# One load and two sets of mask transfers moved between queues in an attention and PReLU kernel

## The chip, the cores and the metric

The kernel runs on one core of a Trainium2 chip. The metric is the device time of one execution in microseconds (us). A core has five engines that matter here: TensorE (PE, with its weight loads shown as PEld), VectorE (DVE), ScalarE (ACT), GpSimd (POOL) and SyncE (SP), which issues transfers. Each engine works through its own instructions in order; an instruction that waits holds up everything behind it on that engine. Transfers (DMA) are issued by SP, ACT or POOL and run on 16 DMA engines that all of them share.

## The reference

Two stages follow each other. The first is linear attention with decay in blocks of 64 positions, for 4 batches, 8 heads, 768 positions and 64 elements a head; the second is a two-layer feed-forward network on the 3072 resulting rows of 512 elements, with 2048 hidden elements and a PReLU between the layers.

```python
for b in range(nb):
    qb, kb, vb = q[:, :, sl], k[:, :, sl], v[:, :, sl]
    intra = einsum('bhic,bhjc->bhij', qb, kb) * Dmask[None]      # lam ** (i - j), 0 above the diagonal
    intra = einsum('bhij,bhjd->bhid', intra, vb)
    inter = einsum('bhid,bhde->bhie', qb * lam_pow[None], kv_state)
    out[:, :, sl] = intra + inter
    kb_dec = kb * rev_pow[None]
    kv_state = lam_block * kv_state + einsum('bhsd,bhse->bhde', kb_dec, vb)
...
h = x @ w_in
g = maximum(h, 0) + alpha * minimum(h, 0)
return g @ w_out
```

## The kernel before

**Tiling.** The kernel works with blocks of L = 128 positions, two to a window of W = 256. There are NC = 6 chunks: chunk c covers window c // 2 of the batches 2 * (c % 2) and 2 * (c % 2) + 1. A chunk has four attention units, numbered n = 4 * c + 2 * bi + hh, one for each of its two batches (bi) and each half of the heads (hh). So units 16 to 19 are chunk 4, the last but one, and units 18 and 19 its second batch. Chunks 4 and 5 (c >= HC) lay their keys out by halves of a block rather than by even and odd positions, and need their own arrangement of the decay masks.

**One unit.** load brings q and k of a batch in as 32-bit floats (L82; for k of the last chunks in four transfers, L94), load_vh brings v, cast to 16 bits on the way, in two transfers for each half (L335). cast makes 16-bit q and k (L298 on ACT, L300 on VectorE, L302 on POOL), key_decayed multiplies k by its decay (L358), transposes(n, "D") turns q and k with one transposing transfer on SP's queue (L378, tile qkT), decayed multiplies the turned q by its decay on POOL (L422, tile qdT). A cluster(old, new) then runs on PE inter(old) (L442, needs qdT of the old unit), score_products(new) (L460 in the last chunks, L472 before; needs qkT of the new unit), intra(old) (L506) and state_products(new) (L526); masked(new) multiplies the scores by the decay mask on VectorE (L485 in the last chunks, L487 before), attended copies the result on ACT (L298) and states updates the running states (L555).

**The masks of the last chunks.** half_mask(hh) builds the mask for half hh of the heads out of the general one by four transfers from SBUF to SBUF (L257), 64 KB each: 32 rows by 4 by 128 floats, written to every second row. half_mask(0) writes into a fresh tile (hmask). half_mask(1) reads the general mask of the second half and writes over that of the first (dmask), so it must come after masked(14), the last user of that one. later_half(hh) finishes each with a copy on POOL (L264). masked(16) is the first to need the mask of half 0, masked(17) that of half 1.

**Feed-forward.** up(c, f) makes one of 16 groups of 128 hidden elements for the 512 rows of chunk c (four matmuls at L635, a Relu of the negative on ACT at L643, the PReLU on VectorE at L650); down(c, t, part, 4) adds a quarter of the second product for 128 rows (four matmuls at L663), and the last quarter ends with a copy on ACT (L676) and a store on SP's queue (L679). PE alternates between these and the clusters.

**What sets the order.** The order is written out by hand, one call after another (L827 to L1135), then by a table (plan) for chunks 3 to 5. Each call appends its instructions to the engines' queues at that place. The change lies at L1081 to L1121, where the attention of units 11 to 16 is interleaved with down of chunk 1 and up of chunk 2. On SP's queue stand there in turn: the transposes of unit 14, a store, half of q for units 16 and 17, four mask transfers, a store, the transposes of unit 15, q for units 18 and 19, four transfers of k for the same, the transposes of unit 16, a store, four mask transfers, the transposes of unit 17. The tiles of qkT rotate over three buffers, the 32-bit q and k over five.

Of the kernel before, what the change touches and what calls it, by code (L numbers as in the profile page):

```python
# [11 lines left out]
def kernel(  # L12
# [16 lines left out]
    nc = tc.nc  # L29
# [52 lines left out]
    def load(c, bi, x, half=None, queue="S"):  # L82

        pb, b = c // 2, 2 * (c % 2) + bi
        if (c, bi) not in raws:
            raws[c, bi] = {}
        if x not in raws[c, bi]:
            raws[c, bi][x] = raw_pool.tile([128, H, 2 * D], fp32, tag=f"{x}raw", name=f"{x}raw")
        heads = ds(0, H) if half is None else ds(4 * half, 4)
        i = "kqv".index(x)  # L90
        if x == "k" and c >= HC:
            for a in range(2):
                for f in range(2):
                    nc.sync.dma_start(  # L94
                        out=raws[c, bi][x][ds(64 * a, 64), heads, ds(D * f, D)],
                        in_=k[b, heads, ds(pb * W + L * a + 64 * f, 64), :].rearrange("h p d -> p h d"),
                    )
            return
        (nc.gpsimd if queue == "G" else nc.sync).dma_start(  # L99
            out=raws[c, bi][x][:, heads, :],  # L100
            in_=(k, q, v)[i][b, heads, ds(pb * W, W), :].rearrange("h (p e) d -> p h (e d)", e=2),
        )
# [39 lines left out]
    def bank_of(bank, name, dtype=fp32):  # L142
        pool = h_ps_pool if bank == "h" else ps
        return pool.tile([128, CH], dtype, tag=bank, name=name)
# [102 lines left out]
    def half_mask(hh):  # L247

        m = [dmask[:, x].rearrange("p l h a j -> p (l h) (a j)") for x in range(2)]
        if hh == 0:  # L250
            t = raw_pool.tile([128, H, 2 * D], fp32, tag="vraw", name="hmask")
            HM[0] = t.rearrange("p h d -> p (h d)")[:, 0:768].rearrange("p (x j) -> p x j", j=192)
        else:
            HM[1] = m[0]
        for a in range(2):
            for e in range(2):
                nc.sync.dma_start(  # L257
                    out=HM[hh][64 * a + e : 64 * a + 64 : 2, :, 0:L],
                    in_=m[hh][ds(64 * a, 32), :, ds(64 * (1 - e), L)],
                )  # L260

    def later_half(hh):

        nc.gpsimd.tensor_copy(  # L264
            out=HM[hh][:, :, L:192].rearrange("p x (e j) -> p x e j", e=2),
            in_=HM[hh][:, :, 0:L].rearrange("p x (e j) -> p x e j", e=2)[:, :, :, 0:32],
        )
# [28 lines left out]
    def copy_on(eng, out, in_):  # L296
        if eng == "A":
            nc.scalar.activation(out, in_, AF.Copy)  # L298
        elif eng == "V":
            nc.vector.tensor_copy(out=out, in_=in_)  # L300
        else:
            nc.gpsimd.tensor_copy(out=out, in_=in_)  # L302

    def raw_of(n):
        c, bi, hh = units[n]
        return {
            x + "16": t[:, ds(4 * hh, 4), :].rearrange("p h (e d) -> p e h d", e=2)
            for x, t in raws[c, bi].items()
        }

    def cast(n, name, eng):
        t = T.setdefault(n, {})
        if name == "v16":
            t[name] = v_of(n)
            c, bi, hh = units[n]
            copy_on(eng, t[name].rearrange("p h e d -> p h (e d)"), raws[c, bi]["v"][:, ds(4 * hh, 4), :])
            return
        if "qk16" not in t:
            t["qk16"] = half_pool.tile([128, 2, 2, 4, D], fp16, tag="qk16", name="qk16")
        copy_on(eng, t["qk16"][:, int(name == "k16")], raw_of(n)[name])  # L320
# [3 lines left out]
    def v_of(n):  # L324
        c, bi, hh = units[n]
        if (c, bi) not in V:
            V[c, bi] = v_pool.tile([128, H, 2, D], fp16, tag="v16", name="v16")
        return V[c, bi][:, ds(4 * hh, 4)]

    def load_vh(c, bi, a):  # L330

        for n in (4 * c + 2 * bi, 4 * c + 2 * bi + 1):
            T.setdefault(n, {})["v16"] = v_of(n)
        for f in range(2):
            nc.gpsimd.dma_start(  # L335
                out=V[c, bi][ds(64 * a, 64), :, f],
                in_=v[2 * (c % 2) + bi, :, ds((c // 2) * W + L * a + 64 * f, 64), :].rearrange("h p d -> p h d"),
            )
# [11 lines left out]
    def engine(x):  # L350
        return nc.gpsimd if x == "G" else nc.vector

    def key_decayed(n, eng="G"):
        hh = units[n][2]
        kr = raw_of(n)["k16"]
        decay = hdecay if units[n][0] >= HC else kdecay
        kdec = kv_pool.tile([128, 2, 4, D], fp16, tag="kdec", name="kdec")
        engine(eng).tensor_tensor(  # L358
            out=kdec,
            in0=kr,  # L360
            in1=decay[:, ds(4 * hh, 4), :].rearrange("p h e -> p e h").unsqueeze(3).to_broadcast([128, 2, 4, D]),
            op=ALU.mult,
        )
        T.setdefault(n, {})["kdec"] = kdec
# [8 lines left out]
    def transposes(n, eng, decay=True):  # L373

        t = T[n]
        qkT = qkt_pool.tile([128, 2, 2, 2, L], fp16, tag="qkT", name="qkT")
        if eng == "D":
            nc.sync.dma_start(  # L378
                out=qkT.rearrange("p x e h j -> p (x e h) j"),
                in_=t["qk16"].rearrange("p x e h d -> p (x e h d)"),  # L380
                transpose=True,
            )
        else:
            tp = ps.tile([128, 2, 2, 2, L], fp16, tag="tk", name="tp")
            for x in (1, 0):
                for e in range(2):
                    for hp in range(2):
                        nc.tensor.transpose(
                            tp[:, x, e, hp, :],
                            t["qk16"][:, x, e, ds(2 * hp, 2)].rearrange("p l d -> p (l d)"),  # L390
                            ident,
                        )
            copy_on(eng, qkT, tp)
            t["qps"] = tp[:, 0]
        t["qkT"] = qkT
        if decay:
            decayed(n)
# [19 lines left out]
    def decayed(n, eng="G"):  # L417
        c, bi, hh = units[n]
        t = T[n]
        qdT = qkt_pool.tile([128, 2, 2, L], fp16, tag="qdT", name="qdT")  # L420
        p = ds(64, 64) if c < 2 else ds(0, L)
        engine(eng).tensor_tensor(  # L422
            out=qdT[:, :, :, p],
            in0=(t["qps"] if eng == "P" else t["qkT"][:, 0])[:, :, :, p],
            in1=qdecay[:, hh, :, :, p],
            op=ALU.mult,
        )
        t["qdT"] = qdT
# [139 lines left out]
    def cluster(old, new, eng="A"):  # L568

        if old is not None:  # L570
            inter(old)
        if new is not None:
            score_products(new)
        if old is not None:
            intra(old)
        if new is not None:
            state_products(new, kv_acc, old is None)
            masked(new)
        if old is not None:
            attended(old, eng)  # L580
        if new is not None:
            states(new, kv_acc)
# [35 lines left out]
    G = {}  # L618
# [35 lines left out]
    def lhs(c, f, t):  # L654
        return g_of(c, f)[:, t // 2, t % 2, :]

    def down(c, t, part, nparts, bank="op"):
        if part == 0:
            O[c, t] = bank_of(bank, "o_ps")
        o_ps = O[c, t]  # L660
        n = NF // nparts
        for f in range(part * n, part * n + n):
            nc.tensor.matmul(  # L663
                o_ps,
                lhsT=lhs(c, f, t),
                rhs=w_out_sb[:, f, :],
                start=(f == 0),
                stop=(f == NF - 1),
            )
        if part == nparts - 1:  # L670
            store(c, t, o_ps, 0, DM)
            del O[c, t]
# [408 lines left out]
    transposes(14, "D", False)  # L1081
    down(1, 2, 3, 4, "h")
    load(4, 0, "q", 1)
    half_mask(0)
    cast(15, "k16", "G")
    cast(17, "q16", "G")
    load_vh(4, 0, 0)
    cluster(11, 12, "A")
# [7 lines left out]
    key_decayed(17, "G")  # L1096
    up(2, 2, None, "h")
    up(2, 0, None, "tk")
    load(4, 1, "q", None)
    cast(17, "k16", "G")  # L1100
    decayed(14, "G")
    cast(16, "k16", "G")
    load_vh(4, 1, 0)
    cluster(12, 13, "A")
    load(4, 1, "k", None)
    transposes(16, "D", False)
    down(1, 3, 2, 4, "op")
    up(2, 1, None, "h")
    load_vh(4, 1, 1)
    up(2, 15, None, "h")  # L1110
    up(2, 8, None, "tk")
    later_half(0)
    decayed(15, "G")
    key_decayed(16, "G")
    key_decayed(18, "G")
    cluster(13, 14, "A")
    down(1, 3, 3, 4, "op")
    half_mask(1)
    up(2, 10, None, "h")
    up(2, 13, None, "h")  # L1120
    up(2, 11, None, "op")  # L1121
# [116 lines left out]
```

## Time and profile before

| | |
|---|---|
| runs of before, median (lowest to highest) | 207.32 us (206.71 to 207.41), 3 runs |
| profiled execution | 206.72 us |
| its span, first to last instruction | 204.9 us |
| PE busy | 198.6 us, 97% of the span |
| VectorE, POOL, ACT busy | 154.9, 116.1, 113.8 us |
| granted TensorE clock | 1.00 |
| the chain that ended last | PE 86%, DMA 4%, VectorE 3%, SP's issues 3% |

Times in the views are counted from the first instruction. A row of a timeline has the start, the length, the engine, the line of the kernel, the operation, what is written and read, and the count; in brackets stands the engine's idle time just before and what ended it. "SPq" is SP's queue: its rows are the issuing of a transfer, not the transfer. The time "to landing" of a transfer runs from the start of its issue until all of its data is reported written; for some transfers the trace has none.

### The profile page before, as it was taken

Reading aid. Unit: us, or ns where it says so; the run is one execution under the profiler, and the core shown is the slowest. Engines: PE = TensorE matmul, PEld = TensorE weight load, DVE = VectorE, ACT = ScalarE, POOL = GpSimd, SP = SyncE. Lnnn points to the kernel's source line nnn. Section 1 sums busy time; section 2 is a strip of 40 time slices with the busy share of each in tenths; the row PEclk is TensorE's granted clock in tenths of the full one; section 3 lists DMA queues with packets and bytes.
Section 4 is the critical chain, followed back from the end, with each engine's and each line's share of the span. In section 5 each row is a group of like instructions: output and inputs, shape, how many; then the busy total and the mean of one; then the engine's idle time right before and its main releaser. Section 6 shows DMA issues by size and latency. Waiting matters only on the chain.

```text
span 204.9 us, 5641 instructions
## 1 busy us (share of the span) xinstructions
PE 198.6 (97%) x2271; PEld 121.2 (59%) x2271; DVE 154.9 (76%) x289; ACT 113.8 (56%) x212; POOL 116.1 (57%) x145
## 2 busy tenths in 40 slices
PE   7999999999999999999799999999999999999993
PEld 6776445556445465555454554467666666666883
DVE  6988889578789647899977679958888467675831
ACT  7986778144777118656486466654453544534320
POOL 8999893054478991299286957982085040553000
PEclk9999999999999999999999999999999999999999
DMA  5999999997999996899999995381001111011123
GB/s 165 278 196 234 248 264 207 234 293 230 230 261 282 201 231 156 226 154 218 180 242 140 263 151 79 65 128 37 18 0 54 51 54 51 3 51 55 62 88 110
DMA packets 67871, 31.71 MB, mean 155 GB/s; under 512 B 39860, under 2 KB 65604, under 8 KB 67844
## 3 DMA queue, kind: packets, MB, share of 16 engines
q1 hardware_dynamic: 48180, 21.64, 47.2%
q0 software_dynamic: 19360, 9.57, 33.0%
q8 instruction: 18, 0.29, 0.6%
q10 hardware_dynamic: 304, 0.13, 0.2%
q14 instruction: 9, 0.07, 0.1%
HBM read 27.27 MB, written 6.29 MB: 164 GB/s over the span
## 4 chain that ended last, share of the span: by engine, by line
PE 86%; DMA 4%; DVE 3%; SPq 3%; ACT 1%; issue 1%; ACTq 0%
PE h_ps L635 36%; PE o_ps L663 20%; PE o_ps L745 18%; DMA qkT<-qk 4%; PE acc L506 2%; PE s L472 2%; PE acc L442 2%; PE tpx L408 2%; SPq L94 1%; DVE dmask L212 1%; PE s L460 1%; PE acc L526 1%; SPq L378 1%; SPq L99 1%; ACT L190 1%
## 5 line engine op out<-in xcount | busy, mean ns | idle before, releaser
L650 DVE SCALAR_TENSOR_TENSOR g<-m,oma,h_ps 128x512 f16<-128x512 f32 (+1 forms) x98 | 71.4, 736 | 28.7 <-ACT m L643 25.5
L635 PE MATMUL h_ps<-xT,w_in_sb 128*128 128x512 f16 (+1 forms) x392 | 92.0, 375 | 0.0
L643 ACT ACTIVATE m<-h_ps 128x512 f32<-128x512 f32 (+1 forms) x98 | 57.3, 588 | 46.8 <-PE h_ps L635 35.9
L635 PEld LDWEIGHTS <-w_in_sb 128*128 128x128 f16 x392 | 37.6, 98 | 37.0
L663 PE MATMUL o_ps<-w_out_sb,g 128*128 128x512 f16 x192 | 46.8, 380 | 0.0
L745 PEld LDWEIGHTS <-g 128*128 128x128 f16 x296 | 28.2, 98 | 8.2
L663 PEld LDWEIGHTS <-g 128*128 128x128 f16 x192 | 17.6, 98 | 19.4 <-DVE g L650 0.2
L728 POOL TENSOR_TENSOR s<-g 128x512 f16<-128x512 f16 x11 | 12.8, 1168 | 28.4 <-PE o_ps L745 16.1
L487 DVE TENSOR_TENSOR sm<-s,dmask 128x1024 f16<-128x1024 f32 x16 | 19.6, 1222 | 11.7 <-PE s L472 11.7
L298 ACT ACTIVATE xT<-acc 128x512 f16<-128x512 f32 x24 | 14.3, 597 | 24.1 <-PE acc L526 22.1
L422 POOL TENSOR_TENSOR qdT<-qkT,qdecay 128x512 f16<-128x512 f16 (+1 forms) x19 | 20.1, 1065 | 7.9 <-DMA qkT<-qk 4.7
L745 PE MATMUL o_ps<-w_out_sb,g 128*128 128x256 f16 x192 | 24.1, 273 | 0.0
L302 POOL CAST qk<-qraw 128x512 f16<-128x512 f32 x12 | 8.5, 707 | 18.3 <-DMA qraw<-in_q_dram 17.8
L555 DVE SCALAR_TENSOR_TENSOR R<-R,rdecay,acc 128x128 f16<-128x128 f16 x54 | 15.5, 342 | 0.1
L728 POOL TENSOR_TENSOR g<-g 128x512 f16<-128x512 f16 x11 | 13.2, 1199 | 0.9
L777 ACT ACTIVATE o_sb<-o_ps 128x512 f32<-128x512 f32 (+1 forms) x15 | 7.5, 497 | 7.6 <-PE o_ps L745 7.6
L358 POOL TENSOR_TENSOR kdec<-kraw,kdecay 128x512 f16<-128x512 f32 x10 | 10.7, 1082 | 1.1 <-DMA kraw<-in_k_dram 1.0
L335 POOL DMA_DIRECT2D v<-in_v_dram x16 | 11.1, 701 | 0.4 <-issue 0.4
L745 PE MATMUL o_ps<-w_sum,g 128*128 128x256 f16 x88 | 11.3, 273 | 0.0
L780 DVE TENSOR_TENSOR o_sb<-o_sb,o_ps 128x512 f32<-128x512 f32 (+1 forms) x12 | 6.5, 550 | 4.2 <-PE o_ps L745 2.2
L302 POOL CAST qk<-kraw 128x512 f16<-128x512 f32 x9 | 5.5, 614 | 6.9 <-DMA kraw<-in_k_dram 6.9
L506 PE MATMUL acc<-sm,v 64*64 64x128 f16 (+1 forms) x384 | 9.2, 214 | 0.0
(95 smaller groups left out, 219.7 us busy)
## 6 DMA issues: line engine op xcount, KB each, us to landing
out_dram<-o_sb SPq DMA_DIRECT2D x20, 256.0 KB, 2.9
qraw<-in_q_dram SPq DMA_DIRECT2D x6, 512.0 KB, 6.2
w_in_sb<-in_moe_w_in_dram POOLq DMA_DIRECT2D x4, 512.0 KB, 7.9
w_out_sb<-in_moe_w_out_dram POOLq DMA_DIRECT2D x4, 512.0 KB, 10.5
kraw<-in_k_dram SPq DMA_DIRECT2D x16, 128.0 KB, 4.9
kraw<-in_k_dram SPq DMA_DIRECT2D x3, 512.0 KB, 4.2
qraw<-in_q_dram POOLq DMA_DIRECT2D x6, 256.0 KB, 7.1
qraw<-in_q_dram SPq DMA_DIRECT2D x6, 256.0 KB
```

Source lines behind the costliest of these rows:

```text
L298: nc.scalar.activation(out, in_, AF.Copy)
L302: nc.gpsimd.tensor_copy(out=out, in_=in_)
L422: engine(eng).tensor_tensor(out=qdT[:, :, :, p], in0=(t["qps"] if eng == "P" else t["qkT"][:, 0])[:, :, :, p], in1=qdecay[:, hh, :, :, p], ...
L487: nc.vector.tensor_tensor(out=t["sm"].rearrange("p a h x j -> p (a h) x j"), in0=t["s"].rearrange("p a h x j -> p (a h) x j"), in1=mask_of ...
L506: nc.tensor.matmul(o, lhsT=t["v16"][p, 2 * hp + hl, e, :], rhs=x, start=(2 * pb + a == 0 and hp == 0 and e == 0), stop=(e == 1), skip_grou ...
L555: nc.vector.scalar_tensor_tensor(out=R[b, hh, m + 1][:, hp], in0=R[b, hh, m][:, hp], scalar=rdecay[:, 2 * hh + hp : 2 * hh + hp + 1], in1= ...
L635: nc.tensor.matmul(h_ps[:, 0:n] if bi is None else h_ps[:, 0:n].rearrange("p (e j) -> p e j", e=2), lhsT=w_in_sb[:, gi, ts(f, 128)], rhs=x ...
L643: nc.scalar.activation(m[:, 0:n], h_ps[:, 0:n], AF.Relu, scale=-1.0)
L650: nc.vector.scalar_tensor_tensor(out=g, in0=mv, scalar=oma[:, f : f + 1], in1=hv, op0=ALU.mult, op1=ALU.add)
L663: nc.tensor.matmul(o_ps, lhsT=lhs(c, f, t), rhs=w_out_sb[:, f, :], start=(f == 0), stop=(f == NF - 1),)
L728: engine(eng).tensor_tensor(out=out, in0=in0, in1=in1, op=op)
L745: nc.tensor.matmul(t[:, cols], lhsT=x, rhs=w, start=(fresh and f == 0), stop=(last and f == NF // 2 - 1), skip_group_check=True,)
```

## The change

Three things, all in the order or the issuing engine; no arithmetic changes.

- The eight transfers of half_mask are issued by POOL instead of SP.
- The load of q for units 18 and 19 goes behind the transposes of unit 16; the load of k for the same units takes its old place, ahead of them.
- half_mask(0) comes one cast earlier on POOL, behind cast(15, "k16"). On POOL, the second half of v for units 18 and 19, later_half(0) and half_mask(1) now stand behind decayed(15) and key_decayed(16), in the order later_half(0), half_mask(1), load_vh(4, 1, 1), key_decayed(18). cluster(13, 14) is written ahead of these. PE, VectorE and ACT keep the order of their instructions.

```diff
@@ half_mask
         for a in range(2):
             for e in range(2):
-                nc.sync.dma_start(
+                nc.gpsimd.dma_start(
                     out=HM[hh][64 * a + e : 64 * a + 64 : 2, :, 0:L],
                     in_=m[hh][ds(64 * a, 32), :, ds(64 * (1 - e), L)],
                 )
@@ the order written out
     load(4, 0, "q", 1)
+    cast(15, "k16", "G")
     half_mask(0)
-    cast(15, "k16", "G")
     cast(17, "q16", "G")
...
     up(2, 0, None, "tk")
-    load(4, 1, "q", None)
+    load(4, 1, "k", None)
     cast(17, "k16", "G")
     decayed(14, "G")
     cast(16, "k16", "G")
     load_vh(4, 1, 0)
     cluster(12, 13, "A")
-    load(4, 1, "k", None)
     transposes(16, "D", False)
+    load(4, 1, "q", None)
     down(1, 3, 2, 4, "op")
     up(2, 1, None, "h")
-    load_vh(4, 1, 1)
     up(2, 15, None, "h")
     up(2, 8, None, "tk")
-    later_half(0)
     decayed(15, "G")
     key_decayed(16, "G")
+    cluster(13, 14, "A")
+    later_half(0)
+    half_mask(1)
+    load_vh(4, 1, 1)
     key_decayed(18, "G")
-    cluster(13, 14, "A")
     down(1, 3, 3, 4, "op")
-    half_mask(1)
     up(2, 10, None, "h")
```

## The prediction

> **What bounds the kernel now.** I read first where TensorE (PE) idles, since it has the highest busy share. The page gives the sum, and the view of busy time by stage finds the place (its columns: length of the stage, then busy time of PE, PEld, DVE, ACT and POOL with instruction counts, granted clock, DMA share, GB/s).
>
> ```profile
> span 204.9 us, 5641 instructions
> PE 198.6 (97%) x2271; PEld 121.2 (59%) x2271; DVE 154.9 (76%) x289; ACT 113.8 (56%) x212; POOL 116.1 (57%) x145
> ...
> 90.00:99.00 9.00, 9.00 (x137) 4.89 (x136) 8.72 (x17) 6.01 (x11) 8.85 (x12) 1.00 1.79 194
> 99.00:102.00 3.00, 1.73 (x49) 1.16 (x48) 2.77 (x5) 1.12 (x3) 0.00 (x0) 1.00 1.27 225
> 102.00:110.00 8.00, 8.00 (x78) 3.96 (x77) 6.31 (x12) 5.50 (x11) 6.52 (x8) 1.00 1.30 200
> ```
>
> PE has one hole around the change, 3.00 - 1.73 = 1.27 us. The timeline of PE shows what ends it (start, length, instruction; in brackets the idle time before it and its releaser).
>
> ```profile
> 99.22 0.39 PE L442 MATMUL acc<-qdT,R 128*128 128x128 f16 x4
> 100.87 0.37 PE L460 MATMUL s<-qkT 64*64 64x128 f16 x16 [1.27 <-DMA qkT<-qk]
> ...
> 105.85 0.39 PE L442 MATMUL acc<-qdT,R 128*128 128x128 f16 x4
> ```
>
> In cluster(15, 16), inter(15) at L442 ends at 99.22 + 0.39 = 99.61, and score_products(16) at L460 must wait until 100.87 for the transposed q and k of unit 16 (call the transposing DMA of unit n T_n). The chain of waits names that transfer (start, length, what), and the timeline of SP's queue shows what stood ahead of it:
>
> ```profile
> 92.78 8.05 DMA qkT<-qk
> ```
> ```profile
> 82.24 0.44 SPq L99 DMA_DIRECT2D qraw<-in_q_dram  x1
> 82.73 2.63 SPq L257 DMA_DIRECT2D hmask<-dmask  x4
> 85.47 0.54 SPq L679 DMA_DIRECT2D out_dram<-o_sb  x1
> 86.15 1.44 SPq L378 DMA_TRANSPOSE qkT<-qk  x1
> 87.63 1.42 SPq L99 DMA_DIRECT2D qraw<-in_q_dram  x1
> 89.09 3.51 SPq L94 DMA_DIRECT2D kraw<-in_k_dram  x4
> 92.78 2.80 SPq L378 DMA_TRANSPOSE qkT<-qk  x1
> 95.68 0.53 SPq L679 DMA_DIRECT2D out_dram<-o_sb  x1
> 96.31 3.58 SPq L257 DMA_DIRECT2D dmask<-dmask  x4
> 99.99 1.28 SPq L378 DMA_TRANSPOSE qkT<-qk  x1
> ```
>
> T_16 is issued at 92.78 and takes 8.05 us to land, right behind q (512 KB) and four parts of k. The third view is the timeline of GpSimd (POOL), because it makes T_16's input and will carry the mask transfers:
>
> ```profile
> 77.10 0.61 POOL L302 CAST qk<-kraw 128x512 f16<-128x512 f32 x1
> 85.59 0.61 POOL L302 CAST qk<-qraw 128x512 f16<-128x512 f32 x1 [7.88 <-DMA qraw<-in_q_dram]
> ...
> 92.03 0.62 POOL L302 CAST qk<-kraw 128x512 f16<-128x512 f32 x1
> 92.58 2.75 POOL L335 DMA_DIRECT2D v<-in_v_dram  x4
> 95.30 0.43 POOL L264 COPY hmask<-hmask 128x256 f32<-128x256 f32 x1
> 95.66 1.20 POOL L422 TENSOR_TENSOR qdT<-qkT,qdecay 128x512 f16<-128x512 f16 x1
> 96.79 2.06 POOL L358 TENSOR_TENSOR kdec<-kraw,hdecay 128x512 f16<-128x512 f32 x2
> 103.31 0.40 POOL L264 COPY dmask<-dmask 128x256 f32<-128x256 f32 x1 [4.46 <-DMA dmask<-dmask]
> 103.67 2.28 POOL L422 TENSOR_TENSOR qdT<-qkT,qdecay 128x512 f16<-128x512 f16 x2
> ```
>
> cast(16, "k16") ends at 92.03 + 0.62 = 92.65, so T_16 cannot be issued earlier than now; only its 8.05 us can shrink.
>
> **The change part by part.**
>
> *Issues taken from SP.* half_mask(0) leaves SP: 2.63 us in four issues. The output store behind it (85.47) had its data long before, from this copy on ACT, so the store, T_15 and the loads behind it come about 2.7 us earlier:
>
> ```profile
> 81.67 0.60 ACT L676 ACTIVATE o_sb<-o_ps 128x512 f32<-128x512 f32 x1 [0.32 <-PE o_ps L663]
> ```
>
> T_15's own input was cast at 77.10 to 77.71. So: store at about 82.75, T_15 at about 83.4, then the k load (4, 1), which now takes q's place, four issues from about 84.9 to 88.4. SP then waits some 4 us for POOL's cast. Nothing gets faster by that alone, but when T_16 is issued at 92.7 k has had over 4 us to land, and q (4, 1) is behind T_16. T_16 is then alone on SP's queue, with two v transfers on POOL's beside it. The view of L378 gives all other transposes that have a landing time:
>
> ```profile
> DMA to landing us min/median/max: 3.8/5.9/6.4
> ```
>
> T_16 must land within 99.61 - 92.78 = 6.83 us. I take 3.8 to 6.4, so even the slowest of them removes the whole stall: **-1.27 us**. That is also the most the change can give, as PE is full on both sides of the hole.
>
> *half_mask(0) on POOL.* Four issues behind the cast at 77.10, in the 7.88 us in which POOL waits for q (17). The nearest price of an issue on POOL is 2.75 / 4 = 0.69 us, so 77.7 to 80.5: **nothing**, hidden by that wait. Without this cover it would be 2.75 us on POOL. At twice the price it would still end by 83.3.
>
> *q (4, 1) late.* Issued at about 94.1 instead of 87.63. The same load took this long before, in the view of DMA issues for 87 to 88 us:
>
> ```profile
> qraw<-in_q_dram SPq DMA_DIRECT2D x1, 512.0 KB, 6.2
> ```
>
> So it lands at about 100.3. Its first user is cast(18, "q16") on ACT:
>
> ```profile
> 103.09 0.62 ACT L298 ACTIVATE qk<-qraw 128x512 f16<-128x512 f32 x1
> ```
>
> With PE 1.27 us ahead that is 101.8: **nothing**, with 1.5 us to spare. If q landed later, ACT would hold the next Relu behind it. T_17 loses the four masks ahead of it (3.58 us) and gains the q load, so it is issued near 96.2 instead of 99.99. Both bounds are no loss.
>
> *POOL's new order.* This decides the result. From 92.58, at the durations above: two v issues 1.38 (to 93.96), decayed(15) 1.13 (95.09), key_decayed(16) 1.03 (96.12), later_half(0) 0.36 (96.48), four issues of half_mask(1) 2.75 (99.23, the last from 98.54), two v issues 1.38 (100.61), key_decayed(18) 1.03 (101.64), then later_half(1), which waits until the masks have landed, then decayed(16). T_15, issued near 83.4, has landed even at 6.4 us. The first mask issue also waits until masked(14) on VectorE has read the masks that it overwrites, which ends at 92.98 and holds nobody:
>
> ```profile
> 91.76 1.22 DVE L487 TENSOR_TENSOR sm<-s,dmask 128x1024 f16<-128x1024 f32 x1
> ```
>
> The first two steps are earlier than before, as inter(15) needs. v (4, 1)'s second half goes from 94 to about 99.2, which costs nothing: its first use is cluster(17, 18), which stands after another cluster and seven more groups of projections.
>
> How the masks land now, the view of L257 tells (issue times of the second set, then both sets' times to landing):
>
> ```profile
> L257 SPq DMA_DIRECT2D dmask<-dmask x4: 605/633/1559, 96.3 to 99.3; - x4
> ...
> DMA to landing us min/median/max: 3.0/3.8/5.4
> ```
>
> What queues behind later_half(1) is decayed(16), and inter(16), the first step of cluster(16, 17), needs it. PE wants it at 105.85 - 1.27 = 104.58. Let the last mask transfer land x us after its issue at 98.54. Before, the last of them was issued at 99.3 and, by the median of 3.8, landed at 103.1; the copy started 0.2 us later, at 103.31. It takes 0.36 and decayed(16) half of 2.28, that is 1.14. So qdT is ready at 98.54 + x + 1.70 = 100.24 + x, and **PE stalls by x - 4.3 us if that is positive**. With the 1.27 us gained, break-even is x = 5.6.
>
> The trace has no mask transfer issued by POOL. The bounds come from four rows: the masks issued by SP, above, and POOL's v transfers of the same 64 KB (L335) in 85 to 96 us, the same in 106 to 110 us, and in the quiet stretch 120 to 140 us.
>
> ```profile
> L335 POOL DMA_DIRECT2D v<-in_v_dram x8: 684/697/730, 86.2 to 94.6; - x8
> ...
> DMA to landing us min/median/max: 4.0/5.4/7.2
> ```
> ```profile
> v<-in_v_dram POOLq DMA_DIRECT2D x4, 64.0 KB, 4.7
> ```
> ```profile
> DMA to landing us min/median/max: 2.6/2.8/3.0
> ```
>
> So x lies between 2.6 and 7.2. The v transfers of 85 to 96 us ran beside the q and four k loads that the change moves away from there; those of 106 to 110 us ran beside two transposes and k loads, which is what 96 to 102 us will now look like. A mask transfer moves 128 pieces of 512 bytes (32 rows, 4 heads, 128 floats), v 512 pieces of 256 bytes, so it should be nearer to the masks' own 3.8. I take 4.2, between 3.8 and 4.7: **no stall**, by a hair. The ends: x = 2.6 none, x = 7.2 a stall of 2.9.
>
> [...]
>
> *Sum.* -1.27 + 0 = -1.27. The profiled execution of before took 206.72 us (span 204.9 and 1.8 around it), so its counterpart would be 205.45. It is a low one: the median of the runs is 207.32, which gives **206.05**.
>
> **The rivals.**
> 1. *The masks land somewhat late* (x from 4.5 to 5.6): the stall moves 5 us on, to inter(16), and takes 0.2 to 1.3 us of the gain. For: v's medians of 4.7 and 5.4. Against: fewer pieces, and T_16 and k ahead of them are gone. At x = 5.0: -1.27 + 0.7, 206.75.
> 2. *The other side: the masks land late beyond break-even.* Place: later_half(1), with decayed(16) queued behind it on POOL, and inter(16) on PE. Price x - 4.3 less the 1.27; it decides from x = 5.6 on and costs over 0.5% from x = 6.6. For: 7.2 was measured. At 7.2: +1.6, 208.95.
> 3. *Issues on POOL are dearer*, because VectorE holds them up or for the masks' row pattern (every second row is written). At twice 0.69 the last mask starts 2.1 us later: a stall of 2.0 at x = 4.2, +0.7, 208.05. Against: the narrow 684 to 730 ns. [...]
> 4. *T_16 is no quicker*: POOL's cast holds its issue, and it lands after 8.05 us again. Then PE is where it was: 207.3. Against: every other transpose with a landing time landed within 6.4.
>
> **How the numbers follow.** Forecast 0.47; rivals 0.22, 0.16, 0.09, 0.06. About 0.5% (1.04 us) is what a measurement of this kernel can tell from no change. The forecast is over it, by only 0.23 us: faster 0.47, I say 0.48 with a little from rival 1. Slower by more than that: 0.11 of rival 2 and 0.06 of rival 3, 0.17. The rest, 0.35, is within. The predicted time is the forecast's, 206.05. Its own range is 205.3 to 206.6 by the scatter of the runs (206.71 to 207.41); rivals of both signs push the top to 208.2, which leaves out the worst of rival 2 above and little below.
>
> **What would show it.** Right: T_16's landing under 6.8 us and no idle time at L460 of cluster(15, 16); T_15 issued near 83.4, T_17 near 96; the four mask issues on POOL near 0.69 us; POOL's wait before the second L264 shorter than 4.46 us. Wrong: a new hole before L442 of cluster(16, 17), put down to POOL's qdT, with a mask landing of over 4.3 us behind it; or ACT idle before cast(18, "q16") for q; or T_16 still 8 us long.

## The result and the profile after

The change made the kernel slower, which the prediction had given a chance of 0.17.

| | before | after |
|---|---|---|
| median of 20 runs each (lowest to highest) | 206.78 us (206.14 to 209.29) | 208.63 us (207.26 to 212.02) |
| ratio of after to before, 95% interval | | 1.0076 [1.0052, 1.01] |
| profiled execution, its span | 206.72 us, 204.9 us | 208.26 us, 206.5 us |

The ratio is taken over the fast runs alone, without those of the slower state, so it is not the quotient of the two medians (1.009).

The busy time by stage after the change (columns as before: PE, PEld, DVE, ACT, POOL, granted clock, DMA share, GB/s):

```profile
99.00:102.00 3.00, 3.00 (x55) 1.71 (x53) 3.00 (x5) 2.00 (x4) 3.00 (x5) 1.00 1.15 314
102.00:110.00 8.00, 5.91 (x68) 2.99 (x67) 5.03 (x11) 4.63 (x9) 4.45 (x6) 1.00 1.41 205
```

The hole of 1.27 us in 99 to 102 us is closed, and one of 8.00 - 5.91 = 2.09 us stands in the next stretch, which was full. PE's timeline shows where:

```profile
99.70 0.39 PE L442 MATMUL acc<-qdT,R 128*128 128x128 f16 x4
100.07 0.37 PE L460 MATMUL s<-qkT 64*64 64x128 f16 x16
...
107.29 0.38 PE L442 MATMUL acc<-qdT,R 128*128 128x128 f16 x4 [2.09 <-POOL qdT L422]
```

score_products(16) at 100.07 follows inter(15) without idle time; inter(16) at 107.29 waits for POOL's qdT. POOL's timeline shows what held that up:

```profile
79.10 2.23 POOL L257 DMA_DIRECT2D hmask<-dmask  x4
87.11 0.62 POOL L302 CAST qk<-qraw 128x512 f16<-128x512 f32 x1 [5.79 <-DMA qraw<-in_q_dram]
...
97.51 2.20 POOL L257 DMA_DIRECT2D dmask<-dmask  x4
99.70 1.40 POOL L335 DMA_DIRECT2D v<-in_v_dram  x2
101.07 1.10 POOL L358 TENSOR_TENSOR kdec<-kraw,hdecay 128x512 f16<-128x512 f32 x1
105.72 0.40 POOL L264 COPY dmask<-dmask 128x256 f32<-128x256 f32 x1 [3.55 <-DMA dmask<-dmask]
106.08 2.28 POOL L422 TENSOR_TENSOR qdT<-qkT,qdecay 128x512 f16<-128x512 f16 x2
```

later_half(1) waits 3.55 us for the masks, with decayed(16) queued behind it. The last of the four mask issues starts at 99.2 (97.51 + 2.20 less one issue of 0.55) and the copy at 105.72. The view of DMA issues for 98.9 to 99.6 us, which holds the last two, gives 6.5 us from issue to landing, and T_17 beside them:

```profile
dmask<-dmask POOLq DMA_DIRECT2D x2, 64.0 KB, 6.5
qkT<-qk SPq DMA_TRANSPOSE x1, 9.0
```

SP's queue shows when the transposes were issued (T_15 at 84.33, T_16 at 93.75, T_17 at 96.84):

```profile
84.33 1.43 SPq L378 DMA_TRANSPOSE qkT<-qk  x1
85.82 2.77 SPq L94 DMA_DIRECT2D kraw<-in_k_dram  x4
93.75 1.27 SPq L378 DMA_TRANSPOSE qkT<-qk  x1
95.48 0.41 SPq L99 DMA_DIRECT2D qraw<-in_q_dram  x1
96.00 0.73 SPq L679 DMA_DIRECT2D out_dram<-o_sb  x1
96.84 3.36 SPq L378 DMA_TRANSPOSE qkT<-qk  x1
```

T_16 landed in time, by the same view for 93.5 to 95 us:

```profile
qkT<-qk SPq DMA_TRANSPOSE x1, 6.3
```

Where the 1.6 us of span come from: inter(15) stands at 99.70 against 99.22, a shift of 0.48 that is no part of the change (below); from inter(15) to inter(16) it is 7.59 us against 6.63, so +0.96 (2.09 - 1.27 = 0.82 of it is the two holes); the rest of the span is 0.15 longer. The shift of 0.48 was there already at inter of an earlier cluster, 64.90 against 64.42, before anything that the change touches; in the eleven other profiles of this study that matmul stands at 64.54 to 65.14. The profiled execution of before was an early one.

### The profile page after: what moved, and what is told of

Its sections match the earlier page's. It is cut to its first block, busy times and chain, and to the rows that moved or that the text cites. A ratio compares the mean times of both kernels' runs of the same rounds, so it can differ in the third digit from the quotient of the medians.

```text
span 206.5 us, 5641 instructions
## 1 busy us (share of the span) xinstructions
PE 199.5 (97%) x2271; PEld 122.4 (59%) x2271; DVE 155.4 (75%) x289; ACT 113.9 (55%) x212; POOL 120.3 (58%) x153
## 4 chain that ended last, share of the span: by engine, by line
PE 91%; DMA 4%; ACT 1%; POOL 1%; ACTq 0%; issue 0%; DVE 0%; POOLq 0%
PE h_ps L635 38%; PE o_ps L663 20%; PE o_ps L745 17%; DMA qkT<-qk 4%; PE acc L506 3%; PE s L472 3%; PE unread L162 3%; PE acc L442 2%; PE tpx L408 2%; PE acc L526 1%; PE s L460 1%; ACT L190 1%; POOL qdT L422 1%; PE p L745 0%; PE unread L150 0%; PE kv L526 0%
## 5 line engine op out<-in xcount | busy, mean ns | idle before, releaser
L302 POOL CAST qk<-qraw 128x512 f16<-128x512 f32 x12 | 7.4, 616 | 16.1 <-DMA qraw<-in_q_dram 16.0
L358 POOL TENSOR_TENSOR kdec<-kraw,kdecay 128x512 f16<-128x512 f32 x10 | 11.4, 1148 | 0.9 <-DMA kraw<-in_k_dram 0.9
L442 PE MATMUL acc<-qdT,R 128*128 128x128 f16 x80 | 8.4, 219 | 2.3 <-POOL qdT L422 2.1
L442 PEld LDWEIGHTS <-R 128*128 128x128 f16 x80 | 6.2, 98 | 6.5 <-issue 2.4
```

Source lines behind the costliest of these rows:

```text
L442: nc.tensor.matmul(ot[a][:, hp, :].rearrange("p (e j) -> p e j", e=2), lhsT=R[bb, ho, 2 * pbo + a][:, hp].rearrange("p l d -> p (l d)"), r ...
```

## The experiments

All medians are set against runs of before on the same chip (medians 206.8 to 207.2). The letter x is that of the prediction, from the start of the last mask issue to its landing; where the trace has no landing for that transfer, it is the start of POOL's copy less the 0.2 us that the prediction used. The hole is the idle time of PE ahead of inter(16).

| kernel | masks of half 1 by | median us | ratio [95%] | last mask issue | T_17 issued | x | hole |
|---|---|---|---|---|---|---|---|
| before | SP | | 1 | 99.29 | 99.99 | 3.8 | 0 |
| after | POOL | 208.63 | 1.0076 [1.0052, 1.01] | 99.17 | 96.84 | 6.4 | 2.09 |
| after, profiled again | POOL | 209.51 (1 run) | | 98.58 | 96.10 | 6.6 | 1.86 |
| E1 decayed(16) first | POOL | 206.65 | 0.9989 [0.9968, 1.001] | 98.90 | 96.62 | 6.9 | 0, then 0.86 |
| E2 q as before | POOL | 209.35 | 1.0146 [1.0094, 1.0197] | 98.72 | 95.41 | 5.9 | 1.25 |
| E3 half 1 by SP | SP | 206.91 | 0.999 [0.9965, 1.0015] | 97.61 | 99.63 | 6.8 | 1.29 |
| E4 only q moved | SP | 207.04 | 1.0001 [0.9981, 1.0021] | 99.10 | 99.81 | 5.3 | 0.95 |
| E5 half 1 earlier | POOL | 205.97 | 0.9955 [0.9939, 0.9971] | 95.89 | 95.90 | 6.9 | 0 |
| E6 only half 0 on POOL | SP | 206.02 | 0.9955 [0.9931, 0.9979] | 96.85 | 98.11 | 4.2 | 0 |
| E7 only the engine | POOL | 209.84 | 1.013 [1.0091, 1.0168] | 100.34 | 94.63 | 5.0 | 1.97 |
| E9 masks ahead of v | POOL | 205.96 | 0.9955 [0.9923, 0.9987] | 96.92 | 95.75 | 7.7 | 1.48 |
| E10 quarter of the rows | POOL | 207.74 (1 run) | | 98.86 | 96.32 | 6.0 | 1.25 |
| E11 T_17 later | POOL | 205.84 | 0.9955 [0.9936, 0.9974] | 98.43 | 99.62 | 4.4 | 0 |

### E1: decayed(16) ahead of later_half(1)

```diff
-    later_half(1)
     decayed(16, "G")
+    later_half(1)
```

> The changed kernel with decayed(16) ahead of later_half(1) on POOL; nothing else moves. Theory (queue order on POOL): the loss is only that decayed(16) stands behind the copy that waits for the masks. Then the hole of 2.1 us before inter(16) goes, T_17 (landed at 105.86 in the changed kernel) leaves at most 0.5 us before score_products(17), and the time is before's 206.8 less 0.8 to 1.3, ratio 0.994 to 0.996. Rival (the DMA engines are simply overloaded from 96 to 106 us): the hole only moves to score_products(17) with some 2 us, and the time stays at 1.005 or above.

The hole at inter(16) is gone, and PE's timeline has another one half a microsecond behind it, at score_products(17):

```profile
104.92 0.39 PE L442 MATMUL acc<-qdT,R 128*128 128x128 f16 x4
106.16 0.37 PE L460 MATMUL s<-qkT 64*64 64x128 f16 x16 [0.86 <-DMA qkT<-qk]
```

So the queue order on POOL is what carries the masks' lateness to PE. T_17, 9.5 us in flight, was hidden behind that hole and is next; it costs 0.86 us where at most 0.5 was expected. The ratio, 0.9989, lies between those of the theory and the rival.

### E2: q (4, 1) ahead of T_16 again, k behind it

```diff
     up(2, 0, None, "tk")
-    load(4, 1, "k", None)
+    load(4, 1, "q", None)
...
     cluster(12, 13, "A")
+    load(4, 1, "k", None)
     transposes(16, "D", False)
-    load(4, 1, "q", None)
```

> The changed kernel with q (4, 1) loaded ahead of T_16 again and k behind q as before, so that only the masks' engine and POOL's order remain changed. Theory (the 512 KB of q, now sent right ahead of the masks, make them land late): the last mask lands within 4.5 us of its issue instead of 6.4, the hole before inter(16) shrinks below 0.3 us, and, as SP is idle from 89 to 93 anyway, T_16 still lands in time: ratio 0.994 to 0.997. Rival (T_17 and a freeze of the DMA engines do it, not q): landing stays above 6 us, hole 2 us, ratio 1.005 or above.

The masks still take 5.9 us, between the two expectations, with T_17 issued 3.3 us ahead of the last of them: q (4, 1) beside them is not needed for the lateness. That no q is needed is not shown, since the next load of q, 512 KB too, now follows T_17 at 96.89, ahead of the last mask. A second hole comes behind it at 116.53, from VectorE (last section).

### E3: half_mask(1) by SP, the rest as after

```diff
-                nc.gpsimd.dma_start(
+                (nc.gpsimd if hh == 0 else nc.sync).dma_start(
                     out=HM[hh][64 * a + e : 64 * a + 64 : 2, :, 0:L],
```

> The changed kernel with half_mask(1) alone issued by SP again, at the same place of the order; half_mask(0) stays on POOL. SP then issues it behind q (4, 1) and a store, about 97 to 99.5 us, nearly when POOL does in the changed kernel. Theory (the stretch, not the engine, makes the masks late): the last lands 5.5 to 7 us after its issue again, hole before inter(16) 1 to 2.5 us, ratio 1.000 to 1.010. Rival (POOL's own path is the slow one): 3.8 us to landing as in the kernel before, no hole, ratio 0.994 to 0.997.

Issued by SP, the masks are as late (6.8 us, hole 1.29): a late landing does not need POOL. Taken alone this does not clear POOL's way of issuing, as the order on SP's queue also changes: q is now right ahead of the masks in the same queue, and T_17 behind them. E11 settles it: there POOL issues the masks, and they land after 4.4 us.

### E4: before with the exchange of q and k alone

```diff
     up(2, 0, None, "tk")
-    load(4, 1, "q", None)
+    load(4, 1, "k", None)
...
     cluster(12, 13, "A")
-    load(4, 1, "k", None)
     transposes(16, "D", False)
+    load(4, 1, "q", None)
```

> The kernel before with only the loads exchanged: k (4, 1) where q was, q behind T_16; masks on SP and POOL's order as before. My step says that T_16 then lands in 3.8 to 6.4 us and its hole of 1.27 us goes. The second masks on SP stand behind q's 512 KB in the same queue: if they still land within 4.3 us of an issue near 99 us there is no new hole, ratio 0.994 to 0.996; if q delays them as POOL's were delayed, a hole of about 1 to 2 us before inter(16), ratio 1.000 to 1.004. If T_16 is as late as before, ratio 1.000 with the hole at the old place.

T_16 is in time, and the 1.27 us come back as 0.95 at inter(16): with q put behind T_16, the last mask takes 5.3 us instead of 3.8, although SP issues it at the same time as before (99.10 and 99.29). None of its ten runs took less than 206.54 us, and none of the ten of E6, which has no hole, more than 206.51, so this is more than one late execution. Where SP issues the masks behind it, q has a part of its own in the lateness.

### E5: half_mask(1) right behind the first half of v (4, 1)

```diff
     load_vh(4, 1, 0)
...
     up(2, 8, None, "tk")
+    cluster(13, 14, "A")
+    half_mask(1)
     decayed(15, "G")
     key_decayed(16, "G")
-    cluster(13, 14, "A")
     later_half(0)
-    half_mask(1)
```

> The changed kernel with half_mask(1) on POOL directly behind the first half of v (4, 1), ahead of decayed(15) and key_decayed(16): the four issues come some 2.5 us earlier, about 95.0 to 97.2. Theory (landing time counts from the issue): at 6.4 us the last lands at about 103.1, qdT of unit 16 is ready near 104.9, PE wants it near 105.05, no hole, ratio 0.994 to 0.997. Rival (a congested stretch ends at a fixed time whatever the issue): the masks land near 105 again, hole 1.5 to 2 us, ratio 1.003 or above.

The masks take 6.9 us, but from 95.89, and nothing waits for them: the copy starts at 102.92, and PE is busy in all of 95 to 110 us. This is faster than before and after.

### E6: before with half_mask(0) alone on POOL

```diff
-                nc.sync.dma_start(
+                (nc.gpsimd if hh == 0 else nc.sync).dma_start(
...
-    half_mask(0)
     cast(15, "k16", "G")
+    half_mask(0)
```

> The kernel before with half_mask(0) alone moved to POOL, behind cast(15, k16); half_mask(1) on SP, q and k and POOL's order as before. Theory (what frees T_16 is SP's 2.6 us of mask issues, not the order of q): SP is done with q and k by 90, T_16 lands before PE needs it at 100; half_mask(1) is issued by SP from about 95.5, a microsecond earlier than before, and lands by 102.5, so no new hole: ratio 0.994 to 0.997. Rival (q has to go behind T_16): T_16 is late by 0.5 us or more still, ratio 0.998 to 1.001.

The smallest edit does as much as any other. With SP rid of half_mask(0), T_16 is in time although q stays ahead of it. The busy time by stage and POOL's timeline of this kernel:

```profile
95.00:110.00 15.00, 15.00 (x198) 7.95 (x197) 13.65 (x26) 10.21 (x19) 10.98 (x14) 1.00 1.94 193
```
```profile
101.17 0.40 POOL L264 COPY dmask<-dmask 128x256 f32<-128x256 f32 x1 [2.43 <-DMA dmask<-dmask]
101.53 2.29 POOL L422 TENSOR_TENSOR qdT<-qkT,qdecay 128x512 f16<-128x512 f16 x2
```

qdT is there at 101.53 + 1.14 = 102.67, over 2 us before PE wants it at 104.90. The move of q and the new order on POOL were not needed for the gain.

### E7: before with all masks issued by POOL, nothing re-ordered

```diff
-                nc.sync.dma_start(
+                nc.gpsimd.dma_start(
                     out=HM[hh][64 * a + e : 64 * a + 64 : 2, :, 0:L],
```

> The kernel before with all eight mask transfers issued by POOL and nothing re-ordered. half_mask(1) then stands behind both halves of v and key_decayed(18), about 99 to 101 us. Theory (landing takes 5 to 6.5 us in this stretch, on POOL's queue decayed(16) is behind it): the last mask lands near 105.5 to 107, a hole of 1.8 to 3.3 us before inter(16), T_16's hole gone: ratio 1.003 to 1.011. Rival (3.8 us to landing as on SP before): lands near 104.3, hole below 1 us, ratio 0.996 to 0.999.

The masks are issued at 98.68 to 100.34, behind POOL's other work, and land 5.0 us later: later in issue than after, shorter in flight, much the same hole (1.97), and the second hole of E2. That one was not expected, and the ratio, 1.013, is above the theory's 1.011.

### E9: the masks ahead of v (4, 1)

```diff
-    load_vh(4, 1, 0)
...
     half_mask(1)
+    load_vh(4, 1, 0)
     load_vh(4, 1, 1)
```

> The changed kernel with the first half of v (4, 1) moved behind half_mask(1) on POOL, so that the masks are first on POOL's queue of transfers and are issued about 1.4 us earlier, from 96.1 to 98.3. Theory (the masks wait in POOL's queue of transfers behind v, whose own landing takes 5 to 6 us there): time to landing falls to 4.5 us or less, the last lands by 102.3, no hole before inter(16), ratio 0.994 to 0.997. Rival (the transposes in flight and the freeze behind T_16 hold every transfer of the stretch): still 6 us or more, landing near 104.5, a hole of 1 us, ratio 0.999 to 1.004.

Not clear-cut. Eight of its ten runs took 205.5 to 206.3 us, as kernels without a hole do; the profiled one took 207.21 and has a hole of 1.48, with x at 7.7, the longest of all. v ahead of the masks on POOL's queue is then not needed to make them late. With the masks issued this early a hole needs an x above some 6.2 (7.7 - 1.48), so in the eight faster runs x was most likely lower by more than a microsecond: it varies that much from one execution to another. T_16 took only 3.2 us in the profiled execution and landed at 96.1, 0.4 us after T_17 was issued. So T_16 in flight beside T_17 is not needed for a late landing either.

### E10: a quarter of the masks' rows

```diff
-                    out=HM[hh][64 * a + e : 64 * a + 64 : 2, :, 0:L],
-                    in_=m[hh][ds(64 * a, 32), :, ds(64 * (1 - e), L)],
+                    out=HM[hh][64 * a + e : 64 * a + (64 if hh == 0 else 16) : 2, :, 0:L],
+                    in_=m[hh][ds(64 * a, 32 if hh == 0 else 8), :, ds(64 * (1 - e), L)],
```

> After with the four transfers of half_mask(1) cut to 8 of their 32 rows (a quarter of the bytes; three quarters of the mask of half 1 are left out, so units 17 and the later odd ones of these chunks get other scores). Theory A, they wait for other transfers in the 16 engines and their own size hardly matters: the last still takes 5.5 us or more to land, and the hole before inter(16) stays at 1.2 us or more. Rival B, their own pieces take the time: at most 4.3 us, and no hole at L442.

The last two issues, in the view of DMA issues for 98.8 to 99.3 us:

```profile
dmask<-dmask POOLq DMA_DIRECT2D x2, 16.0 KB, 6.1
qkT<-qk SPq DMA_TRANSPOSE x1, 9.0
```

In this execution 16 KB land nearly as late (x 6.0) as 64 KB do (6.4 and 6.6): the time is mostly waiting, not the transfer's own pieces. That takes away the prediction's argument for a value near the masks' own 3.8.

### E11: T_17 held back until the masks are issued

cast(17, "k16"), which T_17 needs, moves behind half_mask(1) on POOL.

```diff
     load(4, 1, "k", None)
-    cast(17, "k16", "G")
...
     half_mask(1)
+    cast(17, "k16", "G")
     load_vh(4, 1, 1)
```

> After with cast(17, "k16") on POOL moved behind half_mask(1), so that T_17 cannot be issued before about 99.7 us (96.84 in after) while the mask transfers are issued 0.6 us earlier, from about 96.9 to 98.5. Nothing else changes on the queues until then. Theory A, the masks land late because two transposes, T_16 and T_17, are in flight with them: the last mask transfer lands within 5.0 us of its issue (6.4 in after), by about 103.5, the hole of 2.1 us before inter(16) at L442 is gone or under 0.3 us; T_17 itself lands near 106 and PE may wait for it at scores(17), L460, by 0.3 to 1.5 us; time 206.0 to 207.5. Rival B, T_17 has no part in it (T_16, q and v alone make the stretch slow): still 6 us or more, landing at 104.5 or later, a hole of 1.3 us or more at L442, time 207.5 or more.

The first theory's landing and hole: x is 4.4 and the hole gone. Nine of ten runs took 205.7 to 206.05 us and one 207.30; the median of 205.84 is just under the theory's range, since PE does not wait for T_17. SP's queue, POOL and PE in turn:

```profile
95.29 0.55 SPq L679 DMA_DIRECT2D out_dram<-o_sb  x1
99.62 1.28 SPq L378 DMA_TRANSPOSE qkT<-qk  x1
```
```profile
96.78 2.20 POOL L257 DMA_DIRECT2D dmask<-dmask  x4
...
103.01 0.40 POOL L264 COPY dmask<-dmask 128x256 f32<-128x256 f32 x1 [1.01 <-DMA dmask<-dmask]
```
```profile
104.90 0.39 PE L442 MATMUL acc<-qdT,R 128*128 128x128 f16 x4
105.21 0.37 PE L460 MATMUL s<-qkT 64*64 64x128 f16 x16
```

With q, v and T_16 where after has them, the copy waits 1.01 us instead of 3.55. T_17, issued 2.8 us later, also lands sooner, at 104.8 against 105.9, and T_16 has landed when it is issued (6.5 us after 93.04, at 99.6): score_products(17) at 105.21 does not wait. Its issue takes SP 1.28 us against 3.36. The masks are issued 0.7 us earlier than in after (98.43 against 99.17), but that is not what helps them: in the second profile of the changed kernel (next) the last of them goes out at 98.58, with T_17 at 96.10, and x is 6.6.

### The changed kernel profiled once more

> The changed kernel as it is, profiled once more, to see how far the landing of the masks varies from one execution to another. If the 6.4 us of the first profile are typical: 5.8 to 7.0 us again, and a hole of 1.5 to 2.7 us before inter(16). If it was one bad execution: under 5.0 us, and a hole under 0.7 us.

SP's queue and POOL:

```profile
96.10 3.57 SPq L378 DMA_TRANSPOSE qkT<-qk  x1
```
```profile
96.93 2.19 POOL L257 DMA_DIRECT2D dmask<-dmask  x4
...
105.35 0.40 POOL L264 COPY dmask<-dmask 128x256 f32<-128x256 f32 x1 [3.77 <-DMA dmask<-dmask]
```

x is 6.6 and the hole 1.86, so the first profile was no exception. This execution took 209.51 us, though, with a shorter hole than the first: its clock dropped (last section).

## Why the prediction was wrong

The mechanism that decided was the one that the prediction named for the other side, and its formula held: a stall of x - 4.3 us at inter(16). With x = 6.4 it gives 2.1, and 2.09 was measured. The steps in their order:

- *Issues taken from SP.* Held. T_15 was issued at 84.33 (near 83.4 forecast, 0.5 of the difference being the early profile of before) and k in one go behind it.
- *T_16.* Held. Its issue was bound by POOL's cast, it landed in 6.3 us (3.8 to 6.4 forecast), and the 1.27 us were gained, with little to spare: in E10 PE waits 0.21 us for it. E6 shows that freeing SP of half_mask(0) was enough for that.
- *half_mask(0) on POOL at nothing.* Held: 79.10 to 81.33, and POOL still idles 5.79 us behind it.
- *q late.* Its own user did not wait, as forecast. What was not forecast is its effect on others: E4's profile puts it at 1.5 us of x, where SP issues the masks behind it.
- *POOL's order and the price of an issue.* Held: 2.20 / 4 = 0.55 us each instead of 0.69, the last at 99.17 (98.54 forecast, 0.5 of it the early profile). Rival 3 is out: no run shows VectorE holding the issues up or twice their price. They were this short although VectorE was busy for all 2.25 us of 97.50 to 99.75, in which they lie; one took 544 to 578 ns.
- *The landing of the masks.* **This step failed**: x taken as 4.2, between 3.8 and 4.7, was 6.4. What the runs showed in its place is T_17. The prediction saw that T_17 would go out near 96.2 instead of 99.99 and costed this at "no loss" for T_17 itself; what it would do to the masks was not priced. It now went out 2.3 us ahead of the last mask issue, where before had it 0.7 us behind. E11 undoes this one thing, and 2 us of x go with it.
- *The choice within the bounds.* The prediction did expect two transposes beside the masks and had a row for that, v in 106 to 110 us with 4.7, but took less, because a mask moves fewer pieces (the 512 pieces of 256 bytes that it gives for v are v as read, 128 KB; 64 KB are written). E10 speaks against the argument. The row was too mild all the same: at 4.7 the stall is 0.4, and the change still gains. Of the rows shown only v in 85 to 96 us, 4.0 to 7.2, reached 6.4, and break-even at 5.6 lay inside it.

The table agrees in part. Where POOL issues the masks, x is 5.9 to 7.7 with T_17 issued up to 3.3 us ahead of the last of them or together with it, 5.0 in E7 with T_17 5.7 us ahead, and 4.4 with T_17 behind them. Where SP issues them, T_17 is always behind: 3.8 and 4.2 with q in its old place, 5.3 and 6.8 with q behind T_16. So T_17 is what made the masks late in after, as E11 shows, but it is not the only thing that can: q right ahead of them in their queue does it too. How much of E3's 6.8 is q and how much is the scatter between executions stays open; each x is from one execution. How T_17 delays the masks stays open as well: in E2 it landed 5.7 us after its issue, not 9, and x was still 5.9.

The size: the holes alone make +0.82 us, yet the medians differ by 1.85. The 14 of the 20 runs of after whose mean granted clock is 0.996 or higher have a median of 207.98, which is +1.20; the six below 0.993 took 209.35 us or more. By these medians about a third of the loss is not the wait but a slower clock, an estimate; one profile shows that clock behind the hole (last section). The remaining 0.4 between 0.82 and 1.20 was not separated; it is within the scatter of x.

## What to carry to other kernels

When a transfer is let out earlier, price it also as traffic: ask which transfer that something waits for will now be in flight with it (x of 6.4 in after with T_17 ahead of the last mask, 4.4 in E11 with T_17 behind). Even a row with much the same company can be too mild (4.7 against 6.4 here), so where the break-even lies within the spread of the nearest rows, as 5.6 did in 4.0 to 7.2, the gain is a bet. Of several edits that go together, try the smallest that removes the wait (here half_mask(0) alone, 0.9955 of before): the others can cost what it gains (1.0076 with all of them). And a copy that waits for a transfer should stand behind the work on its queue that does not need it: in E1 this took away the hole of 2.09 us, though a later wait of 0.86 us came up behind it.

## What the runs showed of the hardware

**A hole of 1.9 us can cost twice.** In the second profile of the changed kernel the granted clock halves a little after the hole. Busy time by stage (the clock is the third number from the end), then PE's timeline:

```profile
106.90:107.80 0.90, 0.88 (x44) 0.76 (x43) 0.09 (x1) 0.00 (x0) 0.90 (x1) 1.00 1.36 268
107.80:108.50 0.70, 0.70 (x10) 0.32 (x4) 0.70 (x1) 0.56 (x1) 0.70 (x2) 0.74 1.32 254
108.50:109.20 0.70, 0.70 (x3) 0.19 (x2) 0.68 (x3) 0.03 (x1) 0.70 (x2) 0.50 1.63 225
...
110.00:111.00 1.00, 1.00 (x4) 0.34 (x3) 0.88 (x2) 0.08 (x1) 1.00 (x3) 0.50 0.20 9
111.00:112.00 1.00, 1.00 (x5) 0.44 (x4) 0.20 (x1) 0.00 (x0) 0.68 (x2) 0.72 1.21 188
112.00:113.00 1.00, 1.00 (x7) 0.41 (x6) 0.05 (x1) 0.60 (x1) 0.00 (x0) 1.00 1.56 118
```
```profile
106.92 0.38 PE L442 MATMUL acc<-qdT,R 128*128 128x128 f16 x4 [1.86 <-POOL qdT L422]
...
107.83 1.62 PE L635 MATMUL h_ps<-xT,w_in_sb 128*128 128x512 f16 x4
109.25 1.91 PE L663 MATMUL o_ps<-w_out_sb,g 128*128 128x512 f16 x4
110.95 1.33 PE L635 MATMUL h_ps<-xT,w_in_sb 128*128 128x512 f16 x4
112.12 1.03 PE L663 MATMUL o_ps<-w_out_sb,g 128*128 128x512 f16 x4
```

Three groups that take 1.03 us at full clock take 1.62, 1.91 and 1.33: 1.77 us more, beside the 1.86 of the hole. In the first profile, with a hole of 2.09, the clock stays at 1.00 in 102 to 110. The stages from 108.5 to 111 have the clock at 0.50; if it is 0.50 or 1.00 at each moment, the 0.74 and 0.72 of the stages at the two ends put it at the half from about 108.1 to 111.6, an estimate. That the hole brought it down is inferred from the runs: a mean clock of 0.992 or less stands in six of the 20 runs of after, two of four of E2 and three of four of E7, whose profiles have holes of 1.25 us or more at inter(16), and in none of the 59 runs of before taken along with the experiments (0.994 at the lowest). It does not do so every time: none of the ten runs each of E3 and E9, with holes of 1.29 and 1.48 us in their profiles, is below 0.996.

**One operation on VectorE took 4.35 us beside POOL.** In E2 and E7, where POOL was late, one subtraction of two SBUF tiles on VectorE took 4.35 us; the one before it took 0.42 and 0.52. VectorE's timeline and then POOL's, of E2:

```profile
109.75 0.42 DVE L711 TENSOR_TENSOR w_sum<-w_out_sb 128x512 f16<-128x512 f16 x1
111.47 4.35 DVE L711 TENSOR_TENSOR w_sum<-w_out_sb 128x512 f16<-128x512 f16 x1
```
```profile
111.22 1.20 POOL L422 TENSOR_TENSOR qdT<-qkT,qdecay 128x512 f16<-128x512 f16 x1
...
114.48 1.05 POOL L358 TENSOR_TENSOR kdec<-kraw,hdecay 128x512 f16<-128x512 f32 x1
115.49 1.34 POOL L728 TENSOR_TENSOR s<-g 128x512 f16<-128x512 f16 x1
```

It begins 0.25 us behind the start of the first of four POOL operations that stand back to back and ends at 115.82, 0.3 us after the last of the four, when a fifth has begun (115.49). The one before it, at 109.75 with its 0.42 us, ran while POOL only issued transfers (108.48 to 111.23). That POOL held the long one is the author's reading of these times; no run tests it. PE's wait for VectorE that follows is the second hole of both kernels, 1.15 us at 116.53 and 117.09, and these two have the slowest medians of the kernels with more than one run.

**Almost all transfers can stop for over a microsecond.** In 97.2 to 98.6 us of after (at most 12 GB/s) and 98.3 to 99.5 us of before (at most 15) almost nothing moves. This is the rate in the view of DMA of before for 96 to 103 us, in 40 slices of 0.175 us:

```profile
GB/s 146 168 152 164 151 167 123 278 159 144 124 155 62 15 0 0 7 9 9 10 67 157 157 141 150 313 399 376 364 312 331 340 343 326 233 200 203 146 149 287
```

It is not needed for the masks to be late. The same line for the second profile of the changed kernel has no slice from 97 to 101 us (the 6th to the 28th) under 45 GB/s, and x is 6.6 there:

```profile
GB/s 279 261 142 59 116 45 59 78 76 205 186 214 277 304 320 322 336 358 394 365 369 354 328 287 200 117 91 76 57 48 10 64 268 307 456 34 378 31 3 34
```

What stops the transfers was not tested.
